# Row-tiled transposes of q and k, 64x128 tiles for the scores and the state's part, and a later place for u's transposes

## The chip, the cores and the metric

The kernel runs on one core of a Trainium2 chip. A core has five engines with instruction queues of their own: TensorE (PE, matrix products; the loading of its stationary operand is listed apart as PEld), VectorE (DVE), ScalarE (ACT), GpSimd (POOL) and SyncE (SP, which only issues transfers here). TensorE writes into PSUM, eight banks of 512 fp32 values for each of 128 partitions, and DVE and ACT read it from there. The metric is the device time of one execution in microseconds (us): 671.15 us as the median of 3 runs (670.82 to 672.76).

## The reference: what is computed

```python
# attention, B=4, H=8, S=768, D=64; a decay lam per head
for b in range(nb):                       # blocks of tokens
    intra = einsum('bhic,bhjc->bhij', qb, kb) * Dmask
    intra = einsum('bhij,bhjd->bhid', intra, vb)
    inter = einsum('bhid,bhde->bhie', qb * lam_pow, kv_state)
    out[:, :, sl] = intra + inter
    kv_state = lam_block * kv_state + einsum('bhsd,bhse->bhde', kb * rev_pow, vb)
# mixer, x = out as (4, 768, 512); rank 32, hidden 2048
h  = x.transpose(0, 2, 1) @ U @ V
u  = x + h.transpose(0, 2, 1)
return u + maximum(u @ w_ch1, 0) @ w_ch2
```

The first part is a causal linear attention with a state per head. The second adds a low-rank mix over the tokens and then a two-layer network over the 512 channels.

## The kernel before, in words

The kernel has three stages. The front stage (about the first 118 us) computes the attention and the low-rank mix, in 24 steps: step `s` is one tile of 128 tokens of one batch, six tiles to a batch (`NT = 6`, `c = s % NT`). The two later stages are the two large products with the weights (lines 733/743 and 866/868/870); they are not touched.

The order in the front stage is written out by hand: a list `pieces` (lines 562 to 584) names the pieces of each step, and every engine executes its own share strictly in that order. No planner moves anything. For step `s` TensorE gets, in this order:

- `prep(s+1)`, through `turn_half` (L355): the 8 heads of q and of k of the next tile, transposed two heads at a time on the full 128x128 array: four transposes into the PSUM bank `pq`, four into `pk`. ACT copies each bank to SBUF (`qt`, `kt`, L358).
- `mix(done)` with `done = s - 7` (L515): one 128x512 product into the bank `pu`; DVE adds it to the tile's attention result (L518). From then on the tile is u.
- At the first tile of a batch only (steps 6, 12, 18): `low(b-1)` (L470), the 24 products of the low-rank part, into `pp`. For batch 0 it lies in bank `pu`, later in bank `pq`. `low_rows` and two later pieces read it: DVE L490 and, behind the state's addition, DVE L496 (for batch 0 ACT copies it away first, L486).
- `intra(s)` (L453): masked scores times v into `px`, on 128x64 tiles; ACT copies it out (L459).
- `state(s)` (L418): decayed k times v into `pkv`, in bank `pk`; DVE adds it to the faded state (L426). Not in the last tile of a batch.
- `scores(s+1)` (L400): the scores of the next tile into the two banks `pss`. Up to step 6 on two 64x128 tiles of the array (rows x columns), after it on four 64x64 tiles.
- `inter(s+1)` (L441): the state's part of the next tile, q scaled (`qs`, by POOL, L383) times the state, into `px`, on four 64x64 tiles. Not in the first tile of a batch, which has no state.
- `turn(done)` (L532): four 128x128 transposes of u into the bank `pt`, and behind them SP's store of u to DRAM. DVE splits the result (L537, L548).

`masked(s+1)` (DVE, L409) multiplies the scores with the decay mask and frees `pss`. `aside` holds steps that prepare weights, mostly on DVE. A one-off beginning (`keep_busy`, `pl`) runs a few products on zeros and spreads `lam`.

fp32 products take two passes through the array, so the profile counts two records for each; transposes have one.

Of the kernel before, what the change touches and what calls it, by code (L numbers as in the profile page):

```python
# [8 lines left out]
FP32 = mybir.dt.float32  # L9
# [5 lines left out]
P = 128  # L15
# [3 lines left out]
def kernel(  # L19
# [28 lines left out]
    nc = tc.nc  # L48

    B, H, S, D = q.shape  # L50
    HP = H // 2
    NT = S // P
    C = H * D
# [9 lines left out]
    TG = N // P  # L63
# [5 lines left out]
    FG = (NS - NT - 1) // TG  # L69
# [24 lines left out]
    u_d = [dram.tile([P, C], FP32, name=f"u_d{s}") for s in range(NS)]  # L94
# [151 lines left out]
    att = att_ctx.enter_context(tc.tile_pool(name="att", bufs=1))  # L246
# [14 lines left out]
    def bank(shape, name, tag):  # L261
        return psa[0].tile(shape, FP32, tag=tag, bufs=2, name=name)
# [3 lines left out]
    raw = {}  # L266

    def parts(s):
        return 2 if s == 0 else 1
# [23 lines left out]
    ident = keep.tile([P, P], FP32, name="ident")  # L293
# [40 lines left out]
    xs = {}  # L334
    st = {}
    kv = {}
    half = [slice(0, D), slice(D, P)]

    def keep_busy(n):

        out = one_bank([P, C], "idle", "pq")
        for i in range(n):
            nc.tensor.matmul(out=out[:, 0:P], lhsT=blank, rhs=blank, start=True, stop=True)  # L343

    qts, kts = {}, {}

    def turn_half(s, a0, name):

        ts, tag = (qts, ("pq", "pt")) if name == "q" else (kts, ("pk", "pu"))
        if a0 == 0:  # L350
            ts[s] = att.tile([P, HP, P], FP32, tag=name + "t", bufs=2, name=name + "t")
        n = HP // parts(s)
        pt = one_bank([P, n, P], "p" + name, tag[a0 > 0])
        for a in range(a0, a0 + n):
            nc.tensor.transpose(  # L355
                out=pt[:, a - a0, :], in_=raw[s, name][:, 2 * a : 2 * a + 2, :], identity=ident
            )
        nc.scalar.copy(ts[s][:, a0 : a0 + n, :], pt)  # L358

    def prep(s):  # L360
        for a0 in range(0, HP, HP // parts(s)):
            for name in "qk":
                turn_half(s, a0, name)
        st[s].update(qt=qts.pop(s), kt=kts.pop(s))
        for name in "qk":
            load_next(name)
# [27 lines left out]
    def scores(s):  # L394
        qt, kt = st[s]["qt"], st[s]["kt"]
        st[s]["pss"] = pss = two_banks("pss", "pss").rearrange("p x (a i) -> p x a i", a=HP)
        for a in range(HP):
            for x in range(2):
                for rows in half if s > NT else [slice(0, P)]:
                    nc.tensor.matmul(  # L400
                        out=pss[rows, x, a, :], lhsT=kt[half[x], a, rows],
                        rhs=qt[half[x], a, :], start=True, stop=True,
                    )

    def masked(s):
        pss = st[s].pop("pss")
# [4 lines left out]
    def state(s):  # L411
        c = s % NT
        if c < NT - 1:
            ks, vr = st[s]["ks"], raw[s, "v"]
            pkv = one_bank([P, HP, D], "pkv", "pk")
            for a in range(HP):
                for x in range(2):
                    nc.tensor.matmul(  # L418
                        out=pkv[half[x], a, :], lhsT=ks[:, a, x, :], rhs=vr[:, 2 * a + x, :],
                        start=True, stop=True,  # L420
                    )
            kv[s + 1] = att.tile([P, HP, D], FP32, tag="kv", bufs=2, name="kv")
            if c == 0:
                nc.vector.tensor_copy(out=kv[s + 1], in_=pkv)
            else:
                nc.vector.tensor_tensor(out=kv[s + 1], in0=pkv, in1=st[s]["faded"], op=ALU.add)  # L426
        del st[s]
        del raw[s, "v"]
        load_next("v")

    def inter(s):

        st[s]["px"] = both = two_banks("px", "px")
        px = both[:, :, 0 : HP * D].rearrange("p x (a e) -> p x a e", a=HP)
        if s % NT == 0:
            return

        for a in range(HP):
            for x in range(2):
                for t in range(2):  # L440
                    nc.tensor.matmul(  # L441
                        out=px[half[t], x, a, :], lhsT=st[s]["qs"][half[x], a, half[t]],
                        rhs=kv[s][half[x], a, :], start=(a == 0), stop=False,
                    )

    def intra(s):
        first = s % NT == 0
# [15 lines left out]

    def low(b):

        tag = "pq" if b else "pu"
        pp = one_bank([P, P], "pp", tag) if b < B - 1 else bank([P, P], "pp", "b2")
        for c in range(NT):
            for g in range(G):
                nc.tensor.matmul(  # L470
                    out=pp[g * R : (g + 1) * R, :], lhsT=u_w[:, c, :],
                    rhs=xs[b * NT + c][:, g * P : (g + 1) * P],
                    start=(c == 0), stop=(c == NT - 1),
                )
        pps[b] = pp
# [44 lines left out]
    uhl, ud, turned = {}, {}, {}  # L520
    hl_at, d_at = [hl_pool], [d_pool]

    def turn(s):

        g, n = divmod(s, TG)
        if n == 0:
            uhl[g] = hl_at[g >= FG].tile([P, 2, CT, N], F32R, tag="hl", name="u_hl")
            ud[g] = d_at[g >= FG].tile([P, CT, N], F32R, tag="d", name="u_d")
        cols = slice(n * P, (n + 1) * P)
        pt = one_bank([P, CT, P], "put", "pt") if g < FG else bank([P, CT, P], "put", "b1")  # L530
        for ct in range(CT):
            nc.tensor.transpose(  # L532
                out=pt[:, ct, :], in_=xs[s][:, ct * P : (ct + 1) * P], identity=ident
            )
        nc.sync.dma_start(out=u_d[s], in_=xs.pop(s))
        t = tmp("ut").rearrange("p (c n) -> p c n", n=P)
        nc.vector.tensor_scalar(t.bitcast(U32), pt.bitcast(U32), HI, None, ALU.bitwise_and)  # L537
        hi, low, diff = uhl[g][:, 0, :, cols], uhl[g][:, 1, :, cols], ud[g][:, :, cols]
        if g >= FG:

            nc.vector.scalar_tensor_tensor(diff, t, 1.0 + E, pt, ALU.mult, ALU.subtract)
            uf = tmp("uf").rearrange("p (c n) -> p c n", n=P)
            nc.scalar.mul(hi, t, E)
            nc.scalar.copy(uf, pt)
            nc.gpsimd.tensor_tensor(out=low, in0=uf, in1=t, op=ALU.subtract)
            return
# [16 lines left out]
    for s in range(NS):  # L563
        b, c = divmod(s, NT)
        done = s - NT - 1
        more = s + 1 < NS
        step = [("prep", s + 1), ("scale", s + 1)] * more + [("fade", s)] * (c == 1)
        step += [("late", s - 1)] * (s in (NT, 3 * NT - 1))
        step += [("mix", done)] * (0 <= done < NS - NT - 1)
        step += [("low", b - 1)] * (c == 0 and b > 0)  # L570
        step += [("low_rows", b - 1)] * (c == 0 and b > 0)
        step += [("intra", s)]
        step += [("next_of_low", b - 1)] * (c == 0 and b > 0)
        step += [("late", s)] * (s < NT - 1 or s == NT) + [("state", s)]
        step += [("next_of_low", b - 1)] * (c == 0 and b > 0)
        step += [("turned", done - 1)] * (done > 0) + [("late", s)] * (done >= 0)
        step += [("next_of_low", b - 1)] * (c == 0 and b > 0)
        step += [("scores", s + 1)] * more
        step += [("aside", s)] * (s >= 2 * NT)
        step += [("inter", s + 1), ("masked", s + 1)] * more  # L580
        step += [("fade", s + 1)] * (more and c > 0)
        step += [("aside", s)] * (s < 2 * NT)
        step += [("turn", done)] * (done >= 0 and done // TG < FG)
        pieces += step
    waiting = {name: list(range(NS)) for name in "qkv"}

    def load_next(name, engine=nc.sync):
# [5 lines left out]
        "prep": prep, "fade": fade, "scores": scores, "masked": masked, "inter": inter,  # L593
        "intra": intra, "state": state,
        "low": low, "low_rows": low_rows, "next_of_low": next_of_low, "mix": mix, "turn": turn,
        "scale": scale, "turned": lambda s: turned.pop(s)(),
    }
    def v_steps():
# [371 lines left out]
```

## Time and profile before

| | |
|---|---|
| median of 3 runs | 671.15 us |
| profiled execution | 671.76 us, its span 669.9 us |
| PE, busy | 663.9 us (99%) |
| DVE, busy | 497.5 us (74%) |
| ACT, busy | 277.5 us (41%) |
| POOL, busy | 112.1 us (17%) |
| first matmul of the large products (L733) | at 118.99 us |
| DVE busy in 50 to 62, 62 to 74, 98 to 110 us | 10.81, 11.55, 11.87 of 12 us |
| transposes of q and k (L355), 192 records | 30.6 us of PE records |
| inter (L441), 640 records | 13.3 us of PE records |
| scores (L400), 656 records | 28.1 us of PE records |

Records of matmuls overlap, since several tiles of the array work at once, and their ends are modelled. What a group costs is therefore read from the start of one group to the start of the next, not from the sum of its records. The timeline gives those starts.

### The profile page before, as it was taken

The page shows a single profiled execution, that of the slowest core. Times are in us where ns is not written, and L with a number is a line of the kernel's source. Part 1 is how long each engine was busy: PE and PEld are TensorE (multiplying, and loading weights), DVE is VectorE, ACT ScalarE, POOL GpSimd, SP SyncE. Part 2 cuts the span into 40 slices and gives each one's busy share as a digit, 9 for nine tenths or more (in the row PEclk, how much of TensorE's full clock was granted, in tenths as well). Part 3 has the DMA queues.
Part 4 walks back from the last instruction along what each step waited for, and adds up shares of the span by engine and source line. Part 5 has one row for each costly group of instructions (what it writes and reads, how often), then busy time and mean ns, then how long its engine had stood idle before and what let it go on. Part 6 is the DMA issues. An engine that isn't in the chain of part 4 may idle for free.

```text
span 669.9 us, 13328 instructions
## 1 busy us (share of the span) xinstructions
PE 663.9 (99%) x5204; PEld 544.5 (81%) x5204; DVE 497.5 (74%) x873; ACT 277.5 (41%) x517; POOL 112.1 (17%) x92
## 2 busy tenths in 40 slices
PE   9999999999999999999999999999999999999997
PEld 8898989788888888888888888888888888888886
DVE  4689989877999777777797265787586775865864
ACT  4675866454655444444454122232322322322320
POOL 4455767240000000000000000030030300300300
PEclk9999999999999999999999999999999999999999
DMA  8999894354776655555577989854363353543421
GB/s 188 219 234 248 212 246 141 102 196 153 262 251 233 215 202 202 201 202 204 204 282 273 326 308 392 282 184 136 95 220 95 118 196 95 160 155 94 163 90 63
DMA packets 131776, 131.29 MB, mean 196 GB/s; under 512 B 81346, under 2 KB 89794, under 8 KB 131714
## 3 DMA queue, kind: packets, MB, share of 16 engines
q1 hardware_dynamic: 130512, 130.05, 61.1%
q8 instruction: 41, 0.67, 0.4%
q10 hardware_dynamic: 1202, 0.39, 0.2%
q14 instruction: 21, 0.17, 0.1%
HBM read 80.09 MB, written 50.33 MB: 195 GB/s over the span
## 4 chain that ended last, share of the span: by engine, by line
PE 97%; DVE 1%; DMA 1%; ACT 0%; issue 0%; DVEq 0%; ACTq 0%
PE pz L733 27%; PE pz L868 13%; PE pz L866 13%; PE pd L743 13%; PE pd L870 13%; PE px L453 4%; PE pss L400 3%; PE put L532 2%; PE pq L355 2%; PE pkv L418 1%; PE pk L355 1%; PE px L441 1%; DMA qraw<-in_q_dram 1%; PE pp L470 1%; PE pu L515 1%; PE idle L343 0%
## 5 line engine op out<-in xcount | busy, mean ns | idle before, releaser
L733 PE MATMUL pz<-u_hl,w 128*128 128x512 f32 x768 | 190.5, 397 | 0.0
L733 PEld LDWEIGHTS pz<-u_hl,w 128*128 128x128 f32 x768 | 144.0, 188 | 35.4 <-issue 0.4
L868 PE MATMUL pz<-w_hl,m 128*128 128x512 f32 x384 | 151.1, 396 | 0.0
L866 PE MATMUL pz<-w_hl,m 128*128 128x512 f32 x384 | 150.9, 396 | 0.0
L870 PE MATMUL pd<-w_d,m 128*128 128x512 f32 x384 | 149.5, 396 | 0.0
L849 ACT ACTIVATE m<-mt 128x512 fp32r<-128x512 f32 x96 | 60.5, 632 | 196.4 <-PE pd L870 140.9
L850 DVE SCALAR_TENSOR_TENSOR m<-rm,m 128x512 fp32r<-128x512 f32 x96 | 71.4, 746 | 53.8 <-ACT m L849 53.5
L895 POOL TENSOR_TENSOR o<-o,u 128x512 f32<-128x512 f32 x20 | 29.9, 1527 | 447.4 <-DVE o L891 447.4
L748 DVE SCALAR_TENSOR_TENSOR r<-pd,r 128x512 f32<-128x512 f32 x96 | 61.8, 686 | 53.6 <-ACT r L739 43.5
L743 PE MATMUL pd<-u_d,w 128*128 128x512 f32 x384 | 98.6, 397 | 0.0
L739 ACT ACTIVATE r<-pz 128x512 f32<-128x512 f32 x96 | 52.2, 596 | 93.2 <-PE pz L733 92.5
L868 PEld LDWEIGHTS pz<-w_hl,m 128*128 128x128 f32 x384 | 72.3, 188 | 17.7
L870 PEld LDWEIGHTS pd<-w_d,m 128*128 128x128 f32 x384 | 72.3, 188 | 17.6
L866 PEld LDWEIGHTS pz<-w_hl,m 128*128 128x128 f32 x384 | 72.3, 188 | 17.6
L743 PEld LDWEIGHTS pd<-u_d,w 128*128 128x128 f32 x384 | 72.1, 188 | 17.3
L851 DVE SCALAR_TENSOR_TENSOR m<-m 128x512 fp32r<-128x512 f32 x96 | 69.1, 721 | 0.9
L848 DVE TENSOR_SCALAR mt<-rm 128x512 uint32<-128x512 uint32 x96 | 46.1, 481 | 26.4 <-DMA rm<-r_d 26.1
L409 DVE TENSOR_TENSOR sm<-pss,mask 128x512 f32<-128x512 f32 x48 | 30.9, 685 | 7.3 <-PE pss L400 7.1
L212 ACT CAST w<-wt 128x512 fp32r<-128x512 f32 x32 | 19.9, 620 | 30.6 <-DVE wt L209 23.4
L383 POOL TENSOR_TENSOR qs<-qt,powq 128x512 f32<-128x512 f32 x20 | 25.9, 1297 | 20.3 <-ACT qt L358 19.8
L453 PEld LDWEIGHTS px<-vraw,sm 128*64 128x64 f32 x768 | 24.6, 137 | 5.5 <-issue 2.3
L453 PE MATMUL px<-vraw,sm 128*64 128x64 f32 x768 | 28.1, 225 | 0.1
(88 smaller groups left out, 682.1 us busy)
## 6 DMA issues: line engine op xcount, KB each, us to landing
r_d<-r SPq DMA_DIRECT2D x96, 256.0 KB, 2.4
rm<-r_d SPq DMA_DIRECT2D x96, 256.0 KB, 2.7
words<-in_moe_w_ch_dram SPq DMA_DIRECT2D x30, 512.0 KB, 4.5
w_d<-w SPq DMA_DIRECT2D x16, 768.0 KB, 3.3
w_hl<-w_d SPq DMA_DIRECT2D x16, 512.0 KB, 6.3
vraw<-in_v_dram SPq DMA_DIRECT2D x24, 256.0 KB, 5.0
u_d<-x_nat SPq DMA_DIRECT2D x24, 256.0 KB, 3.7
u<-u_d SPq DMA_DIRECT2D x24, 256.0 KB, 4.0
```

What stands on the lines that cost most here:

```text
L453: nc.tensor.matmul(out=px[half[t], x, a, :], lhsT=sm[:, x, a, half[t]], rhs=vr[:, 2 * a + x, :], start=(first and a == 0), stop=(a == HP - 1),
L733: nc.tensor.matmul(out=acc[g][0], lhsT=w[:, n, ct, :], rhs=uhl[g][:, n, ct, :], start=(ct == 0 and n == 0), stop=(ct == CT - 1 and n == 1),)
L739: nc.scalar.mul(rs[g], acc[g][0], 4096.0 + 1.0)
L743: nc.tensor.matmul(out=acc[g][1], lhsT=w[:, 2, ct, :], rhs=ud[g][:, ct, :], start=(ct == 0), stop=(ct == CT - 1),)
L748: nc.vector.scalar_tensor_tensor(rs[g], acc[g][1], 4096.0, rs[g], ALU.mult, ALU.add)
L848: nc.vector.tensor_scalar(t.bitcast(U32), r.bitcast(U32), HI, None, ALU.bitwise_and)
L849: nc.scalar.activation(out=m[:, 0], in_=t, func=AF.Relu)
L850: nc.vector.scalar_tensor_tensor(m[:, 1], r, 0.0, hi, ALU.max, ALU.subtract)
L851: nc.vector.scalar_tensor_tensor(m[:, 2], hi, E, low, ALU.mult, ALU.subtract)
L866: nc.tensor.matmul(out=pz, lhsT=m[:, 0, cols], rhs=hl[:, 0], start=first, stop=False)
L868: nc.tensor.matmul(out=pz, lhsT=m[:, 1, cols], rhs=hl[:, 1], start=False, stop=end)
L870: nc.tensor.matmul(out=pd, lhsT=m[:, 2, cols], rhs=dd, start=first, stop=end)
```

## The change

Four things are changed; all other code, the loads and the large products stay.

1. `turn_parts` takes the place of `turn_half`. Each transpose of 128 tokens becomes two of 64 tokens, on the two row tiles of the array (64 rows, 128 columns); their results go to two banks. q and k of a tile share one pair of banks, `pqk`. ACT still makes two copies of 128x512.
2. `scores` uses the 64x128 tiles in all steps, and `inter` has 8 products on 64x128 tiles in place of 16 on 64x64 tiles. The transposes that follow `inter` work on the same shape of tiles.
3. u's transposes (`turn`) move from the end of step `s` to the next step, behind `prep`. The store of u to DRAM keeps its place, as a piece `store` of its own.
4. Banks: `pkv` lies in `pqk` now, `pp` (batches 0 to 2) in `pss`, `idle` in `pt`, `pl` in `pqk`; the second half of the very first tile's transposes goes to `pss`.

```diff
-    def turn_half(s, a0, name):
-        ts, tag = (qts, ("pq", "pt")) if name == "q" else (kts, ("pk", "pu"))
+    def turn_parts(s, a0):
+        n = HP // parts(s)
         if a0 == 0:
-            ts[s] = att.tile([P, HP, P], FP32, tag=name + "t", bufs=2, name=name + "t")
-        n = HP // parts(s)
-        pt = one_bank([P, n, P], "p" + name, tag[a0 > 0])
-        for a in range(a0, a0 + n):
-            nc.tensor.transpose(
-                out=pt[:, a - a0, :], in_=raw[s, name][:, 2 * a : 2 * a + 2, :], identity=ident
-            )
-        nc.scalar.copy(ts[s][:, a0 : a0 + n, :], pt)
+            for ts, name in ((qts, "qt"), (kts, "kt")):
+                ts[s] = att.tile([P, HP, P], FP32, tag=name, bufs=2, name=name)
+        pt = two_banks("pqk", "pss" if a0 else "pqk")[:, :, 0 : 2 * n * D]
+        pt = pt.rearrange("p t (n a i) -> p t n a i", n=2, a=n)
+        for i, name in enumerate("qk"):
+            for a in range(n):
+                for t in range(2):
+                    nc.tensor.transpose(
+                        out=pt[:, t, i, a, :],
+                        in_=raw[s, name][half[t], 2 * (a0 + a) : 2 * (a0 + a) + 2, :],
+                        identity=ident[half[t], half[t]],
+                    )
+        for i, ts in enumerate((qts, kts)):
+            nc.scalar.copy(
+                ts[s][:, a0 : a0 + n, :].rearrange("p a (t i) -> p t a i", t=2), pt[:, :, i]
+            )
@@ scores
-                for rows in half if s > NT else [slice(0, P)]:
-                    nc.tensor.matmul(
-                        out=pss[rows, x, a, :], lhsT=kt[half[x], a, rows],
-                        rhs=qt[half[x], a, :], start=True, stop=True,
-                    )
+                nc.tensor.matmul(
+                    out=pss[:, x, a, :], lhsT=kt[half[x], a, :], rhs=qt[half[x], a, :],
+                    start=True, stop=True,
+                )
@@ state
-            pkv = one_bank([P, HP, D], "pkv", "pk")
+            pkv = two_banks("pkv", "pqk")[:, 0, 0 : HP * D].rearrange("p (a e) -> p a e", a=HP)
@@ inter
-                for t in range(2):
-                    nc.tensor.matmul(
-                        out=px[half[t], x, a, :], lhsT=st[s]["qs"][half[x], a, half[t]],
-                        rhs=kv[s][half[x], a, :], start=(a == 0), stop=False,
-                    )
+                nc.tensor.matmul(
+                    out=px[:, x, a, :], lhsT=st[s]["qs"][half[x], a, :],
+                    rhs=kv[s][half[x], a, :], start=(a == 0), stop=False,
+                )
@@ low
-        tag = "pq" if b else "pu"
-        pp = one_bank([P, P], "pp", tag) if b < B - 1 else bank([P, P], "pp", "b2")
+        pp = two_banks("pp", "pss")[:, 0, 0:P] if b < B - 1 else bank([P, P], "pp", "b2")
@@ turn, and the order of the pieces
+    def store(s):
+        nc.sync.dma_start(out=u_d[s], in_=xs[s])
-        nc.sync.dma_start(out=u_d[s], in_=xs.pop(s))
+        if g >= FG:
+            store(s)
+        del xs[s]
         step += [("late", s - 1)] * (s in (NT, 3 * NT - 1))
+        step += [("turn", done - 1)] * (done > 0 and (done - 1) // TG < FG)
         step += [("mix", done)] * (0 <= done < NS - NT - 1)
...
-        step += [("turn", done)] * (done >= 0 and done // TG < FG)
+        step += [("store", done)] * (done >= 0 and done // TG < FG)
@@ the beginning
-        out = one_bank([P, C], "idle", "pq")
+        out = one_bank([P, C], "idle", "pt")
-    pl = one_bank([P, H], "pl", "pt")
+    pl = two_banks("pl", "pqk")[:, 0, 0:H]
```

On DVE, ACT, POOL and SP the instructions keep their order, the two copies of a tile's transposes (now 128x2x4x64) included. On PE only the groups named above change shape or place.

More of the change, by code (lines that the diff above doesn't have):

```diff
@@ L345 @@
     qts, kts = {}, {}
-    def turn_half(s, a0, name):
-        ts, tag = (qts, ("pq", "pt")) if name == "q" else (kts, ("pk", "pu"))
+    def turn_parts(s, a0):
+        n = HP // parts(s)
         if a0 == 0:
-            ts[s] = att.tile([P, HP, P], FP32, tag=name + "t", bufs=2, name=name + "t")
-        n = HP // parts(s)
-        pt = one_bank([P, n, P], "p" + name, tag[a0 > 0])
-        for a in range(a0, a0 + n):
-            nc.tensor.transpose(
-                out=pt[:, a - a0, :], in_=raw[s, name][:, 2 * a : 2 * a + 2, :], identity=ident
+            for ts, name in ((qts, "qt"), (kts, "kt")):
[13 more added lines that the diff above has]
+                ts[s][:, a0 : a0 + n, :].rearrange("p a (t i) -> p t a i", t=2), pt[:, :, i]
             )
-        nc.scalar.copy(ts[s][:, a0 : a0 + n, :], pt)
     def prep(s):
         for a0 in range(0, HP, HP // parts(s)):
-            for name in "qk":
-                turn_half(s, a0, name)
+            turn_parts(s, a0)
         st[s].update(qt=qts.pop(s), kt=kts.pop(s))
@@ L595 @@
         "low": low, "low_rows": low_rows, "next_of_low": next_of_low, "mix": mix, "turn": turn,
+        "store": store,
         "scale": scale, "turned": lambda s: turned.pop(s)(),
```

## The prediction

> **What bounds the kernel now.** I read the page first, the busy times and the chain that ended last:
>
> ```profile
> PE 663.9 (99%) x5204; PEld 544.5 (81%) x5204; DVE 497.5 (74%) x873; ACT 277.5 (41%) x517; POOL 112.1 (17%) x92
> ...
> PE 97%; DVE 1%; DMA 1%; ACT 0%; issue 0%; DVEq 0%; ACTq 0%
> ```
>
> TensorE's queue sets the end, also in the front stage. Whatever lengthens or shortens the front on PE moves all that follows, so the sum is made of PE time up to the first product of L733 at 118.99 us. Next the PE timeline, here of one whole step (start, us of records, group):
>
> ```profile
> 42.12 1.10 PE L400 MATMUL pss<-qt,kt 64*64 64x128 f32 x32
> 43.04 0.64 PE L441 MATMUL px<-kv,qs 64*64 64x64 f32 x32
> 43.62 0.66 PE L532 MATMUL put<-ident,x_nat 128*128 128x128 f32 x4
> 44.11 0.60 PE L355 MATMUL pq<-ident,qraw 128*128 128x128 f32 x4
> 44.55 0.60 PE L355 MATMUL pk<-ident,kraw 128*128 128x128 f32 x4
> 44.90 0.47 PE L515 MATMUL pu<-vp 128*128 128x512 f32 x1
> 45.30 1.15 PE L453 MATMUL px<-vraw,sm 128*64 128x64 f32 x32
> 46.28 0.64 PE L418 MATMUL pkv<-vraw,ks 128*64 128x64 f32 x16
> 46.85 1.10 PE L400 MATMUL pss<-qt,kt 64*64 64x128 f32 x32
> ```
>
> A step takes 46.85 - 42.12 = 4.73 us with no gap. I count in rounds, one record on every tile of the array at once. L453: 16 rounds in 0.98 us, less 0.05 for its first load: 58 ns, at 64 moving columns. L355: 4 in 0.44: 109 ns at 128. L418: 8 rounds of 58 ns are 0.464 of its 0.57, so a change of tile shape costs 0.106. Third, the weight loads by form (12 to 58 us; busy, mean ns):
>
> ```profile
> L441 PEld LDWEIGHTS px<-kv,qs 64*64 64x64 f32 x320 | 5.8, 134 | 0.6
> L400 PEld LDWEIGHTS pss<-qt,kt 64*128 64x128 f32 x83 | 5.2, 187 | 0.3
> ...
> L355 PEld LDWEIGHTS pk<-ident,kraw 128*128 128x128 f32 x40 | 4.7, 142 | 0.0
> ```
>
> Beside 110 ns for 32 columns (L470, same view), a load grows by 0.8 ns a column: about 53 ns of loading for 64, 107 for 128. A transpose's load of 128 columns takes 142, like one of 64. The load of the next round runs under the present one, so a round lasts as long as the longer of load and stream. The early steps show the one form in which 128 columns are loaded on row tiles:
>
> ```profile
> 28.61 1.16 PE L400 MATMUL pss<-qt,kt 64*128 64x128 f32 x16
> 29.70 0.69 PE L441 MATMUL px<-kv,qs 64*64 64x64 f32 x32
> ```
>
> 1.09 us less 0.107 (first load) and 0.106 (change of shape) is 8 rounds of 110 ns; I use 111.
>
> Last, what reads `pp`, in DVE's and PE's timelines at steps 12 and 18 (two answers):
>
> ```profile
> 67.11 1.10 PE L400 MATMUL pss<-qt,kt 64*64 64x128 f32 x32
> 67.23 0.42 DVE L424 COPY kv<-pkv 128x256 f32<-128x256 f32 x1
> ...
> 67.69 1.25 DVE L496 TENSOR_TENSOR vp<-pp,p_h 32x128 fp32r<-32x128 f32 x4
> ```
>
> ```profile
> 96.39 1.10 PE L400 MATMUL pss<-qt,kt 64*64 64x128 f32 x32
> ...
> 96.97 1.25 DVE L496 TENSOR_TENSOR vp<-pp,p_h 32x128 fp32r<-32x128 f32 x4
> ```
>
> DVE finishes with `pp` at 68.94 and 98.22, 1.83 us after the next scores began. Today nobody minds.
>
> **What the skill says.** The Trainium skill's "TensorE: Matmul & The Clock Gate", section "LDWEIGHTS (loading the stationary operand)", prices a load at its columns / 1.2 ns whatever its rows: 53 and 107 ns, as the trace has it. The same page's "Terms" calls the transposes' load four times faster for fp32; the trace shows twice (142 against 187, of which some 84 is not loading). "TensorEngine Tiling (Array Packing)", "Restrictions", says column tiling takes this mode away; the new transposes use all 128 columns, and no run here shows it on row tiles. Its "Key Properties" has a change of mode drain the array: the 0.106 above.
>
> **The change part by part.**
>
> *Transposes.* Before, 8 rounds of 109 = 0.872 us a tile. After, 16 transposes, two at once, are 8 rounds with 64 moving columns and a fast load of about 57: 8 x 58 = 0.464. Gain 0.408. Bounds: 58, and 111 if on row tiles the load runs as the scores' does (loss 0.016). I take 58, since the load's rate shows no dependence on rows (64*64 and 128*64 both 134 to 138).
>
> *inter.* Before, 8 rounds of 58 = 0.464. After, 8 products of two passes on two tiles are again 8 rounds, now with 128 columns to load for 64 to stream: bound by loads, 8 x 111 = 0.888. Loss 0.424. Bounds 58 and 111; I take 111, which the early scores pay for the same load.
>
> *Scores* after step 6: 8 x 111 + 0.107 for 8 x 109 + 0.053: loss 0.070.
>
> *Changes of shape.* In a full step three before (to 128x64, to 64x64, to 128x128) and three after (128x64, 64x128, 128x128 for u): no gain. In steps 1 to 5, without u, four become two: gain 0.21.
>
> A full step thus loses 0.424 + 0.070 - 0.408 = 0.086 us. A step 1 to 5 goes from 2.74 (28.61 to 31.35) to 0.107 + 0.888 + 0.888 + 0.464 + 0.106 = 2.45: gain 0.29, at most 0.2 after the wait for the mask (1.2 to 2.5 us behind the scores' start, against intra at 2.45).
>
> *Edits at nothing.* ACT's copies stay 0.58 each and may start after q's part; ACT has them done some 3.5 us after the scores' start, `pkv` in `pqk` needs them at 3.4 (early steps; up to 0.1 uncovered) or 4.2. u's later place delays DVE's L537 to L518 by some 0.9 us, into idle time before them; PE reads their result a step later. The store keeps its place in SP's queue, loads theirs. `idle`, `pl`, and the first tile's second half in `pss` (scores there need all four ACT copies) precede the wait for qraw at 17.46, which takes early gains anyway.
>
> *pp in pss, step 6.* `low` must now wait for `masked(6)`, which runs on DVE behind 2.9 us of weight work from 34.03 to 35.32. The early gain reaches DVE as about 0.8 (0.39 from the transposes after qraw's arrival, 0.2 for each of two steps), so `pp` can start at 35.37 - 0.8 = 34.57, against 34.55 before. All early gains end in this wait: net 0, bounds -0.3 and +0.4.
>
> *Steps 7 to 11.* In step 7 `pu` waits for ACT (L505) and hides the loss; then four steps x 0.086 = +0.34.
>
> *Step 12.* Scores(13) must wait until L496 has read `pp`, and behind it on PE stand inter, the next transposes, everything. DVE works without a gap from the mask to L496, so it is late by what PE is: end at 68.94 + 0.34, plus 0.07 to hand over: 69.35 for 67.11. Now +2.24 (PE would be ready at 66.9: `pp` from the mask's end at 63.85, then 1.45 + 0.98 + 0.57). The gain of 0.41 on the transposes in this step vanishes in the wait.
>
> *Steps 13 to 17.* 5 x 0.086: +2.67. *Step 18.* Likewise: 98.22 + 2.67, less 0.35 that DVE waits today for `pp` and `pkv` (0.13 and 0.22), plus 0.07: 100.61 for 96.39: +4.22. *Steps 19 to 22.* +0.34. *Step 23* has inter but no transposes after it: +0.49. **Sum +5.1 us**: the profiled execution goes from 671.76 to 676.9 (span 675.0), and as that execution lies 0.6 over the median of the runs, the median from 671.15 to 676.2.
>
> **The rivals.**
>
> *A, inter's loads don't bind* (not slower). If two row tiles load 128 columns under 64 streamed ones at 58 ns, 14 steps after 7 save 0.424 each: 5.1 - 5.9 = -0.8, 670.4. The scale is linear: no loss below 65 ns a round, within 0.3% (about 2 us, what a measurement of this kernel can tell) below 83. Against it: the 110 ns of the early scores are a little above the 109 of a pure stream, as a load-bound round would be, but there both are long, so the trace doesn't separate them.
>
> *B, the transposes' fast load is lost on row tiles.* 111 ns a round: +0.424 in some 14 steps that PE bounds (8 to 11, 13 to 18, 19 to 22): +5.9, so 682.1. For it: no row-tiled transpose in the trace. Against: loads at equal columns cost the same at 64 and 128 rows.
>
> *C, the wait for pp is short.* If DVE reached L496 right behind PE's state, the two waits (1.9 and 1.55) vanish and the two steps keep their 0.34 from the transposes: 5.1 - 1.9 - 1.55 - 0.68 = +1.0, 672.1. Against: DVE's 11.55 of 12 us there, and seven groups from the mask (L409) to L424 ahead of L496 in its order.
>
> *D, further cost*: PE idle for over 2 us twice may lower its clock, which the skill's clock page (Part 1) puts at half after some 3.4 us of idleness; the trace shows no such gap. Or DVE's lateness reaches intra through the mask, with one buffer. 1 to 4 us more: 678 to 681.
>
> **How the numbers follow.** My case 0.58, B 0.14, D 0.10, C 0.08, A 0.10. The predicted time is that of my case, 676.2, whose own range is 674.3 to 678 (0.4 at step 6, 0.5 in each wait, 15 ns on inter's rounds). The range leaves out A and a part of C and of B's upper side: 672.0 to 682.6. Faster by over 0.3% needs A and a small wait: 0.03. Within 0.3%: most of A and of C: 0.14. Slower: 0.83.
>
> **What would show it.** Right: the 8 transposes of q (L358 then) start 0.23 before those of k; L446 takes 0.89 from its start to the next group's; loads of `px<-kv,qs` near 187 ns, of the transposes near 142; PE waits on DVE L500 (L496 before) of about 2.4 and 1.6 us at the scores of tiles 13 and 19, nowhere else over 0.5 but before `pp`; first L744 product at 124. Wrong: inter's group at 0.5 to 0.6 (A), transposes at 0.9 a tile (B), no wait at the two scores (C), a stage clock below full (D).

## The result, and the profile after

The changed kernel takes 681.8 us (median of 4 runs, 680.85 to 682.37) where the kernel before takes 671.68 (670.82 to 672.76): a ratio of 1.0148, 95% interval 1.0128 to 1.0169. It is slower by 10.1 us; 5.1 were forecast. The time lies in the range that was given, but above 678, where the likeliest case's own range ended. The profiled execution went from 671.76 to 681.63 us, its span from 669.9 to 679.8. From the page, busy times and the chain that ended last:

```profile
PE 666.0 (98%) x4804; PEld 547.6 (81%) x4804; DVE 497.8 (73%) x873; ACT 277.8 (41%) x517; POOL 111.9 (16%) x92
...
PE 95%; DVE 3%; ACT 1%; DMA 1%; issue 0%; ACTq 0%; DVEq 0%
```

DVE's share of the chain rose from 1 to 3%: PE now waits for it. The first product of the large weights (L744, L733 before) starts at 128.83 us for 118.99. These 9.84 us are the whole loss, since from there to the end of the span the kernels take 550.9 and 551.0. The table has it by stretches between the starts of the scores (PE timeline; a stretch "step s" runs from scores(s) to scores(s+1)):

| stretch | before, us | after, us | more | forecast |
|---|---|---|---|---|
| start to scores(6) | 32.44 | 32.81 | +0.37 | -0.8 |
| steps 6 and 7 | 9.68 | 10.86 | +1.18 | +0.8 |
| steps 8 to 11 | 18.47 | 18.81 | +0.34 | +0.34 |
| step 12 | 6.52 | 9.22 | +2.70 | +1.90 |
| step 13 | 4.75 | 6.41 | +1.66 | +0.09 |
| steps 14 to 17 | 18.68 | 18.70 | +0.02 | +0.34 |
| step 18 | 5.85 | 7.51 | +1.66 | +1.55 |
| step 19 | 4.74 | 6.27 | +1.53 | +0.09 |
| steps 20 to 22 | 14.38 | 14.41 | +0.03 | +0.26 |
| step 23 to L744 | 3.48 | 3.83 | +0.35 | +0.49 |

A whole step, in the PE timeline after the change (start, us of records, group):

```profile
48.55 1.16 PE L406 MATMUL pss<-qt,kt 64*128 64x128 f32 x16
49.54 1.01 PE L446 MATMUL px<-kv,qs 64*128 64x64 f32 x16
50.38 0.42 PE L358 MATMUL pqk<-ident,qraw 64*128 64x64 f32 x8
50.63 0.42 PE L358 MATMUL pqk<-ident,kraw 64*128 64x64 f32 x8
50.98 0.66 PE L539 MATMUL put<-ident,x_nat 128*128 128x128 f32 x4
51.39 0.47 PE L519 MATMUL pu<-vp 128*128 128x512 f32 x1
51.79 1.15 PE L458 MATMUL px<-vraw,sm 128*64 128x64 f32 x32
52.77 0.64 PE L424 MATMUL pkv<-vraw,ks 128*64 128x64 f32 x16
53.34 1.16 PE L406 MATMUL pss<-qt,kt 64*128 64x128 f32 x16
```

The step takes 4.79 us, against 4.73. `inter` needs 0.84 from its start to the next group's; the transposes 0.25 for q and 0.35 for k, the change of shape in it. The loads on 12 to 58 us, by form (busy, mean ns):

```profile
L446 PEld LDWEIGHTS px<-kv,qs 64*128 64x128 f32 x144 | 9.0, 188 | 0.2 <-issue 0.2
...
L358 PEld LDWEIGHTS pqk<-ident,kraw 64*128 64x128 f32 x80 | 3.5, 139 | 0.0
```

`inter`'s loads of 128 columns take 188 ns, and the row-tiled transposes keep their fast load, at 139. So the tile shapes cost what was forecast, and the steps between the waits are not where the loss is. It is around tiles 13 and 19 (timeline of PE, two stretches; in brackets the idle time before the group and what ended it):

```profile
65.34 1.52 PE L474 MATMUL pp<-x_nat,u_w 128*32 128x128 f32 x48 [0.39 <-DVE sm L415]
66.79 1.15 PE L458 MATMUL px<-vraw,sm 128*64 128x64 f32 x32
67.77 0.64 PE L424 MATMUL pkv<-vraw,ks 128*64 128x64 f32 x16
71.70 1.90 PE L406 MATMUL pss<-qt,kt 64*128 64x128 f32 x16 [3.29 <-DVE vp L500]
73.38 1.82 PE L446 MATMUL px<-kv,qs 64*128 64x64 f32 x16
74.98 0.57 PE L358 MATMUL pqk<-ident,qraw 64*128 64x64 f32 x8
...
78.11 1.16 PE L406 MATMUL pss<-qt,kt 64*128 64x128 f32 x16
```

```profile
104.32 1.16 PE L406 MATMUL pss<-qt,kt 64*128 64x128 f32 x16 [1.80 <-DVE vp L500]
105.31 1.13 PE L446 MATMUL px<-kv,qs 64*128 64x64 f32 x16
106.23 0.65 PE L358 MATMUL pqk<-ident,qraw 64*128 64x64 f32 x8
106.66 0.64 PE L358 MATMUL pqk<-ident,kraw 64*128 64x64 f32 x8
107.23 1.11 PE L539 MATMUL put<-ident,x_nat 128*128 128x128 f32 x4
```

Two things are to be seen. Before each of these scores PE stands idle, for 3.29 and 1.80 us, until DVE's L500 has read `pp` out of `pss`. And behind the wait the same groups take longer: scores 1.68 from start to start for 1.00, `inter` 1.60 for 0.84, u's transposes 0.77 for 0.41. The same time cut into stretches of one microsecond, around both places (behind the length come the busy us of PE, PEld, DVE, ACT and POOL with their counts of instructions, then PE's granted clock, the DMA share and GB/s):

```profile
71.00:72.00 1.00, 0.30 (x4) 0.30 (x6) 0.58 (x2) 0.96 (x3) 0.09 (x1) 0.97 0.62 226
72.00:73.00 1.00, 1.00 (x14) 1.00 (x14) 0.00 (x0) 0.47 (x1) 1.00 (x1) 0.50 0.06 18
...
74.00:75.00 1.00, 1.00 (x14) 1.00 (x14) 0.92 (x2) 0.00 (x0) 0.00 (x0) 0.50 0.00 0
75.00:76.00 1.00, 1.00 (x20) 0.93 (x20) 0.00 (x0) 0.10 (x1) 0.00 (x0) 0.83 0.00 0
```

```profile
106.00:107.00 1.00, 1.00 (x22) 1.00 (x20) 0.82 (x2) 0.00 (x0) 0.00 (x0) 0.53 0.07 16
107.00:108.00 1.00, 1.00 (x11) 0.88 (x8) 0.00 (x0) 0.66 (x2) 0.00 (x0) 0.50 0.02 5
...
109.00:110.00 1.00, 1.00 (x32) 1.00 (x30) 0.97 (x3) 0.50 (x3) 0.28 (x1) 0.76 0.17 36
```

The clock is halved for about 3.4 us each time: a value of 0.97 means that 0.06 of that microsecond ran at half, so, worked out from the slices, the half clock lasts from 71.94 to 75.34, and from 106.06 to 109.48. All four runs have a mean clock of 0.995 or 0.996, so this is not one unlucky execution. Steps 13 and 19 lose 1.6 and 1.5 us by it.

The other new place is step 6 (PE timeline):

```profile
33.81 0.41 PE L358 MATMUL pqk<-ident,qraw 64*128 64x64 f32 x8
34.05 0.41 PE L358 MATMUL pqk<-ident,kraw 64*128 64x64 f32 x8
35.92 1.52 PE L474 MATMUL pp<-x_nat,u_w 128*32 128x128 f32 x48 [1.46 <-DVE sm L415]
```

### The profile page after: what moved, and what is told of

The parts are those of the page before. It is cut to its first block, busy times and chain, and to the rows that moved or that the text cites. A ratio compares the mean times of both kernels' runs of the same rounds, so it can differ in the third digit from the quotient of the medians.

```text
span 679.8 us, 12534 instructions
## 1 busy us (share of the span) xinstructions
PE 666.0 (98%) x4804; PEld 547.6 (81%) x4804; DVE 497.8 (73%) x873; ACT 277.8 (41%) x517; POOL 111.9 (16%) x92
## 4 chain that ended last, share of the span: by engine, by line
PE 95%; DVE 3%; ACT 1%; DMA 1%; issue 0%; ACTq 0%; DVEq 0%
PE pz L744 27%; PE pz L879 13%; PE pz L877 13%; PE pd L754 13%; PE pd L881 13%; PE pss L406 4%; PE px L458 3%; PE px L446 3%; PE put L539 2%; PE pqk L358 2%; PE pkv L424 1%; DVE sm L415 1%; PE pu L519 1%; PE pp L474 1%; DMA kraw<-in_k_dram 1%; ACT qt L364 0%
## 5 line engine op out<-in xcount | busy, mean ns | idle before, releaser
L744 PE MATMUL pz<-u_hl,w 128*128 128x512 f32 x768 | 190.3, 397 | 0.0
L744 PEld LDWEIGHTS pz<-u_hl,w 128*128 128x128 f32 x768 | 144.0, 188 | 35.3 <-ACT r L750 0.3
L406 PE MATMUL pss<-qt,kt 64*128 64x128 f32 x384 | 29.5, 296 | 6.0 <-DVE vp L500 5.1
L406 PEld LDWEIGHTS pss<-qt,kt 64*128 64x128 f32 x384 | 24.7, 197 | 7.9 <-DVE vp L500 5.4
```

The source lines that it names most:

```text
L406: nc.tensor.matmul(out=pss[:, x, a, :], lhsT=kt[half[x], a, :], rhs=qt[half[x], a, :], start=True, stop=True,)
L744: nc.tensor.matmul(out=acc[g][0], lhsT=w[:, n, ct, :], rhs=uhl[g][:, n, ct, :], start=(ct == 0 and n == 0), stop=(ct == CT - 1 and n == 1),)
```

## The experiments

Times are medians; each kernel is compared with the kernel before on the same chip (671.7 to 672.9 us there).

**Is it the hold of `pp` in `pss`?** The first experiment changes the condition in `low_rows`, so that ACT copies `pp` away for batches 1 and 2 too, as it does for batch 0, and L500 reads the copy:

```diff
-        if b == 0:
+        if b < B - 1:
```

> The changed kernel, but the low-rank result of batches 1 and 2 is first copied out of pss by ScalarE (four copies of 32x128, 0.26 us each), as batch 0 has it; DVE then reads the copy. Theory (two holds of pss, and the clock halved for 3.4 us after each): the scores of tiles 13 and 19 start right behind the state's part, no clock below full between 70 and 112 us, and the 2.7 + 1.6 + 1.7 + 1.5 us that steps 12 and 18 lost are gone: about 674.5. Rival (DVE is the bound of these steps, the hold only shows it): DVE is as late as before, the wait moves to the mask or to pp, and at most 2 to 3 us come back: 679.

Measured: 675.79 us, ratio 1.0075 (1.0054 to 1.0096); from scores(6) to the first large product 89.70 us for 96.02. All waits of PE between 30 and 122 us (in all, times, longest):

```profile
PE pp L474 <- DVE sm L415: 2.0, 3, 1.5
PE px L446 <- DVE kv L430: 0.9, 1, 0.9
```

The waits at the scores are gone, and the clock is 1.0 throughout. A part of them comes back one group later, where `inter` of tile 13 waits 0.87 for the state that DVE is late with; step 13 takes 6.16 us for the 4.80 of the whole steps behind it. So the hold, with what follows from it, is worth some 6 of the 10 us.

The second does the same to the kernel before: only `pp` of batches 0 to 2 is put into `pss`, everything else stays.

```diff
-        tag = "pq" if b else "pu"
-        pp = one_bank([P, P], "pp", tag) if b < B - 1 else bank([P, P], "pp", "b2")
+        pp = two_banks("pp", "pss")[:, 0, 0:P] if b < B - 1 else bank([P, P], "pp", "b2")
```

> The kernel before, with pp (batches 0 to 2) in pss and nothing else changed. Theory: the scores of tiles 13 and 19 wait 1.9 us each for DVE, pp of tile 6 waits 0.8 us for the mask: +4.4, and the clock may halve after each stretch of 1.9 us without products, 1.5 us more each: between 676 and 679. Rival (the hold costs only in combination with the new shapes): +1, 672.7.

Measured: 676.35 us, 1.0061 (1.004 to 1.0082), first large product at 123.01 for 118.99 us. PE waits 0.8 before `pp` of step 6, then 2.2 and 1.8 at the scores of tiles 13 and 19; steps 6, 12 and 18 take 0.90, 1.47 and 1.74 longer than before, 4.1 in sum. The clock stays full: the hold alone costs 4 us.

**Is it the clock?** The third keeps the waits of the changed kernel and fills them: 13 and 7 products of the identity with itself into the free bank `pt`, ahead of the scores of tiles 13 and 19. Their results are used by nobody.

```diff
+    def fill(s):
+        out = one_bank([P, C], "idle", "pt")
+        for i in range(13 if s == 2 * NT else 7):
+            nc.tensor.matmul(out=out[:, 0:P], lhsT=ident, rhs=ident, start=True, stop=True)
...
+        step += [("fill", s)] * (s in (2 * NT, 3 * NT))
         step += [("scores", s + 1)] * more
...
```

> The changed kernel, with 13 and 7 products of the identity with itself (about 2.9 and 1.5 us) put into TensorE's two waits ahead of the scores of tiles 13 and 19. They add no result. Theory (the idle stretch halves the clock afterwards, and the half clock costs 1.6 and 1.5 us): both waits keep their ends (scores at 71.7 and 104.3 or a little earlier), the clock stays at 1.0 throughout, and 3 us come back: 678.8. Rival (the slow stretches have another cause, such as the matmuls' operands or transfers): no change or up to 1 us more: 682 to 683.

Measured: 679.06 us, 1.0116 (1.01 to 1.0131). PE timeline of step 12 to 13:

```profile
69.22 3.17 PE L348 MATMUL idle<-ident 128*128 128x128 f32 x26
72.59 1.16 PE L411 MATMUL pss<-qt,kt 64*128 64x128 f32 x16 [0.21 <-DVE vp L505]
73.59 1.01 PE L451 MATMUL px<-kv,qs 64*128 64x64 f32 x16
```

The scores still start 9.23 us behind those of tile 12 (9.22 in the changed kernel), so the wait is as long as it was; but scores and `inter` have their usual lengths again, and the first large product comes 3.09 us sooner behind scores(6). Useless work makes the kernel faster, by 3.1 us in the trace and 2.7 in the medians: so much of the loss is the clock.

**Why is DVE late in step 12?** The forecast wait was 2.4, the measured one 3.29. One row of DVE's timeline differs (the changed kernel; 0.68 us in the kernel before), and POOL's timeline shows what runs beside it:

```profile
65.11 1.74 DVE L191 SCALAR_TENSOR_TENSOR wf<-m,sc 128x512 f32<-128x512 f32 x1
```

```profile
65.03 1.27 POOL L390 TENSOR_TENSOR qs<-qt,powq 128x512 f32<-128x512 f32 x1
```

L191 and POOL's scaling of q both read two operands in SBUF. POOL starts 0.08 us sooner and ends at 66.30; L191 ends 0.55 after that, as if it had begun its 0.68 about there. In the seven other kernels below and above in which `qs` starts ahead of L191, by 0.07 to 0.23 us, it is the same: L191 ends 0.54 to 0.56 us behind `qs`. The Trainium skill's "SBUF — State Buffer", section "SBUF: two separate sides", says that a DVE operation with two SBUF inputs and a POOL operation that reads SBUF share a port pair as an exclusive lock: who starts first has it to the end, and the other waits in full. Before, `qs` started 3.55 us behind scores(12), after L191 was done; now that q's transposes stand ahead of u's, it starts 2.55 behind, just where L191 (2.6 to 2.8 behind) begins. The test swaps POOL's two instructions of that step, so that `qs` comes behind the waiting `ks`:

```diff
     def scale(s):
+        if s == 2 * NT + 1:
+            scale_k(s + 1)
         if s % NT > 0:
...
-        if s + 1 < NS:
+        if s + 1 < NS and s != 2 * NT + 1:
             scale_k(s + 1)
```

> The changed kernel with POOL's two instructions of tile 13's preparation in the other order: first ks of tile 14, which waits until about 68.5 us, then qs of tile 13, so that qs no longer starts just ahead of DVE's L191 in step 12. Nothing else is changed; inter of tile 13 still finds its qs in time if that is done by about 71. Theory that L191 is held up by qs: L191 takes 0.68 to 0.76 us instead of 1.74, DVE is through with pp about 1.0 earlier (70.6), the wait at the scores of tile 13 falls from 3.29 to about 2.3, and those scores start at about 70.7 instead of 71.7. Time: 680.8 if TensorE's clock is halved after that wait as before, 679.2 if a wait of 2.3 there no longer brings the half clock. Rival, that L191 is slow because of what else moves at that time (transfers, its own operands): it stays at 1.7, the wait at 3.3, time 681.8.

Measured: 678.7 us (678.29 to 679.89), 1.009 (1.0068 to 1.0112). DVE's timeline, and PE's:

```profile
66.12 0.68 DVE L191 SCALAR_TENSOR_TENSOR wf<-m,sc 128x512 f32<-128x512 f32 x1
```

```profile
71.66 1.16 PE L407 MATMUL pss<-qt,kt 64*128 64x128 f32 x16 [2.24 <-DVE vp L501]
72.65 1.01 PE L447 MATMUL px<-kv,qs 64*128 64x64 f32 x16
```

L191 is back at 0.68 and the wait is shorter by 1.05, step 12 now 8.17 us long. That `qs` holds up L191 is shown, and with it the size of the wait. (In this execution all lies some 1.3 us later from the second tile on.) In the profiled execution the clock stayed full after both waits, the unchanged one of 1.80 us too, which no theory had expected; that gave another 3.1 us in steps 13 and 19. It is not sure to do so: two of the four runs have a mean clock of 0.997, which fits one half clock of 3.4 us.

**Is moving u's transposes free?** Only the move and the piece `store`, applied to the kernel before:

```diff
...
+        step += [("turn", done - 1)] * (done > 0 and (done - 1) // TG < FG)
         step += [("mix", done)] * (0 <= done < NS - NT - 1)
...
-        step += [("turn", done)] * (done >= 0 and done // TG < FG)
+        step += [("store", done)] * (done >= 0 and done // TG < FG)
```

> The kernel before, with u's transposes behind those of q and k of the next step, and the store as a piece of its own; nothing else. Theory (the move costs nothing, DVE has the idle time): the full steps stay at 4.73 us and the time within 0.3% of the kernel before. Rival (DVE gets u later and passes it on to the mask or to pp): PE waits of 0.3 us and more a step, +4.

Measured: 674.48 us, 1.0034 (1.002 to 1.0049); the profiled execution had 672.76, its first large product at 120.05, 1.06 later than before. So the move is not free. The six runs go from 672.51 to 674.88, and two of them have a mean clock of 0.996; the trace shows one of the fastest, and explains only a part of the 2.8 us of the medians. Whole steps stay at 4.74. DVE's timeline and PE's, step 12 to 13:

```profile
63.00 1.64 DVE L191 SCALAR_TENSOR_TENSOR wf<-m,sc 128x512 f32<-128x512 f32 x1
```

```profile
68.30 0.69 PE L441 MATMUL px<-kv,qs 64*64 64x64 f32 x32 [1.22 <-DVE kv L424]
69.49 0.66 PE L355 MATMUL pq<-ident,qraw 128*128 128x128 f32 x4 [0.49 <-DVE vp L496]
```

The same collision, without any new tile shape: `qs` starts at 62.80, L191 takes 1.64, and what DVE is late with now holds up `inter`. In all kernels of this study it goes the same way: L191 took 1.59 to 1.75 wherever `qs` had started first, 0.68 to 0.76 wherever it had not; and where L191 came first by 0.17 us, in the two kernels with 64x64 scores below, it was `qs` that took 1.73 and 1.74 for 1.28.

**Do `inter`'s loads bind?** The kernel before with `inter` alone on 64x128 tiles:

```diff
-                for t in range(2):
-                    nc.tensor.matmul(
-                        out=px[half[t], x, a, :], lhsT=st[s]["qs"][half[x], a, half[t]],
-                        rhs=kv[s][half[x], a, :], start=(a == 0), stop=False,
-                    )
+                nc.tensor.matmul(
+                    out=px[:, x, a, :], lhsT=st[s]["qs"][half[x], a, :],
+                    rhs=kv[s][half[x], a, :], start=(a == 0), stop=False,
+                )
```

> The kernel before, with inter alone on 64x128 tiles (8 products in place of 16). Theory (128 columns of weights to load bound a round of 64 streamed ones at 111 ns): inter's group takes 0.89 us in place of 0.46, and behind scores on 64x64 tiles one more change of shape and a longer first load come to it, 0.2 us: 0.6 us in each of 15 steps, about +9: 680.5. Rival A (a load hides under the streams of the other row tile, 58 ns a round): only the change of shape, +1.5 to +3: 673.5.

Measured: 680.99 us, 1.0141 (1.0123 to 1.0159). PE timeline:

```profile
49.52 1.11 PE L440 MATMUL px<-kv,qs 64*128 64x64 f32 x16
50.56 0.66 PE L531 MATMUL put<-ident,x_nat 128*128 128x128 f32 x4
```

`inter` takes 1.04 us for 0.58, and a whole step 5.31 for 4.73. The 0.58 are 8 rounds of 111 for 58 ns (0.424), one more change of shape and a longer first load. Rival A falls.

**Can step 6 be mended?** `pp` of batch 0 back in the bank `pu`, in the changed kernel:

```diff
-        pp = two_banks("pp", "pss")[:, 0, 0:P] if b < B - 1 else bank([P, P], "pp", "b2")
+        if b == 0:
+            pp = one_bank([P, P], "pp", "pu")
+        else:
+            pp = two_banks("pp", "pss")[:, 0, 0:P] if b < B - 1 else bank([P, P], "pp", "b2")
```

> The changed kernel, but the low-rank result of batch 0 lies in the bank pu, as before the change. Theory: the wait of 1.46 us at step 6 is pp's wait for the mask's reading of pss; without it pp runs inside that time and intra of step 6 starts at about 36.0, not 37.37; the rest follows 1.4 us earlier: 680.4. Rival (the mask itself is late, and intra needs it as well): intra waits for the mask instead, less than 0.4 us comes back: 681.5.

Measured: 680.25 us, 1.0133 (1.0115 to 1.0151). Step 6 takes 4.59 us for 6.11, but step 7 5.48 for 4.75, because `inter` of tile 7 now waits 0.81 for the state from DVE. Only 0.8 is left of 1.5; DVE, which prepares weights just there, is what binds. The time fell by more than that: the wait of 3.29 at tile 13 was not followed by a half clock in this execution (step 13 4.81), that of 1.80 at tile 19 was (6.27).

Both repairs together, the one of the first experiment and this one:

> The changed kernel with both repairs: ScalarE copies pp out for batches 1 and 2, and pp of batch 0 lies in pu. Theory: what is left against the kernel before is 0.09 for each full step (about 1.3), 0.35 at step 23, 0.05 in each early step and the waits of 0.4, 0.2 and 0.9 for mask and state: about +3, 675. Rival (the repairs cost what they gain, since DVE is late): as with the copy alone, 676.

Measured: 674.81 us (12 runs), 1.0036 (1.0022 to 1.005). What is left are two waits of `inter` for DVE (0.81 and 0.87), 0.6 before `pp`, and a step 22 of 5.34 us for 4.80.

**Can the shapes be had without `inter`'s loss?** `scores` and `inter` on 64x64 tiles as before, in the changed kernel:

```diff
-                nc.tensor.matmul(
-                    out=pss[:, x, a, :], lhsT=kt[half[x], a, :], rhs=qt[half[x], a, :],
...
+                for rows in half:
+                    nc.tensor.matmul(
+                        out=pss[rows, x, a, :], lhsT=kt[half[x], a, rows],
...
-                nc.tensor.matmul(
-                    out=px[:, x, a, :], lhsT=st[s]["qs"][half[x], a, :],
...
+                for t in range(2):
+                    nc.tensor.matmul(
+                        out=px[half[t], x, a, :], lhsT=st[s]["qs"][half[x], a, half[t]],
...
```

> The changed kernel with scores and inter on four 64x64 tiles in all steps; the transposes on row tiles, u's place and the banks stay. Theory (the transposes gain 0.41 a step, inter and scores lose 0.42 and 0.07, a change of shape between inter and the transposes costs 0.11): a full step falls from 4.80 to about 4.42, and about 5 us come back, the holds of pss and the half clocks staying: 677. Rival (DVE, busy for 93% of these steps, is the next bound): PE waits at the mask or at pp instead, less than 2.5 us comes back: 679.5.

Measured: 678.85 us (675.17 to 680.71, 10 runs), 1.0091 (1.007 to 1.0113). In the profiled execution whole steps take 4.5 to 5.0 us, one 6.5, because PE stands idle where nothing is late ("issue"), once for 1.6 us; seven of the ten runs have a mean clock of 0.997. The same shapes with both repairs and with `pkv` of the first five tiles in `pu`:

```diff
+            if s < NT - 1:
+                pkv = one_bank([P, HP, D], "pkv", "pu")
+            else:
+                pkv = two_banks("pkv", "pqk")[:, 0, 0 : HP * D]
```

> Both repairs, pkv of tiles 0 to 4 in the free bank pu, and scores and inter on 64x64 tiles: what is kept of the change is the transposes on row tiles and u's later place. Theory: 0.30 a step under the kernel before (0.41 of the transposes less one change of shape), 16 to 20 steps, less the waits for the mask at pp: -3 to -5, 668. Rival (DVE becomes the bound): the step stays near 4.7 and the time within 1 us of 671.7.

Measured: 675.31 us (12 runs), 1.0046 (1.003 to 1.0062), 7 us above what the theory had said, with such gaps in the middle of a group:

```profile
75.18 0.57 PE L452 MATMUL px<-kv,qs 64*64 64x64 f32 x21 [1.01 <-issue]
```

By the counts in the timeline these kernels have 133 records of matmuls in a whole step, the kernel before 125, the changed one 101. The next has 117: both repairs, `pkv` likewise, `scores` on 64x128 and only `inter` on 64x64:

> Both repairs, pkv of tiles 0 to 4 in pu, the transposes on row tiles, scores on 64x128 tiles, inter on 64x64 tiles: 32 fewer records of matmuls and loads a step than with the scores on 64x64 tiles. Theory (the gaps put down to issue there came from the number of TensorE's instructions in a stretch with busy DMA engines): no gap put down to issue over 0.3 us on PE, a full step of 4.60 to 4.68 and 671 to 673. Rival (they come from the changes of tile shape, of which this has as many): gaps as before, 674 to 676.

Measured: 672.96 us (20 runs), 1.0021 (1.0013 to 1.0028). No gap of this kind between 30 and 122 us, whole steps of 4.72. So the gaps don't come from changing the tile shape within a step, which this kernel does more often; they appear with the larger number of instructions. What holds PE there isn't shown. This is the best version found, and it is no faster than the kernel before. The L191 collision (1.59) is still in it, and `inter` waits 0.9 for DVE; it was not run with the swap on POOL.

With `inter` on 64x128 in it too, that is the changed kernel with both repairs and `pkv` of five tiles in `pu`:

> Both repairs, and pkv of tiles 0 to 4 in the free bank pu; the shapes are those of the changed kernel. Theory (pkv's four waits of 0.3 us for ScalarE's copy of kt come from its place in pqk): steps 1 to 4 last 4.05 us in place of 4.34, and up to 1.2 us come back, as far as the mask of step 6 passes them on: 673.8. Rival (the mask or the loads of k bound these steps): nothing, 674.8.

Measured: 674.71 us, 1.0043 (1.0028 to 1.0058), no better than without the `pkv` edit (674.81). The edit shows what the early steps are worth: they fall from 4.34 to 3.98 us as long as the loads keep up, and then

```profile
32.49 1.15 PE L462 MATMUL px<-vraw,sm 128*64 128x64 f32 x32 [1.31 <-DMA vraw<-in_v_dram]
```

## Why the prediction was right and wrong

In short, the two mechanisms of the sum came as told: `inter`'s loads bind, and PE waits twice for `pp`. Three of its terms failed. The clock behind the waits stood at nothing and cost 3.0 us. Moving u's transposes stood at nothing and cost 0.8 in step 12. And the early steps, which were to gain 0.8 and so to pay for `pp`'s wait in step 6, lost 0.4. That the time still lies in the range is luck: its upper end had been set for rival B, which did not come.

*The tile shapes: right.* `inter` loses what its loads cost (0.84 measured for 0.89), the transposes' fast load holds on row tiles, and a whole step is longer by 0.065 (4.795 for 4.73) where 0.086 was forecast. Rivals A and B fall, A by an experiment of its own, B by the 139 ns. (The prediction's "twice" compares single loads. A product in fp32 has two of them in these views and a transpose one, so by the prediction's own figures it is 2 x 103 against 58 ns, some 3.5 times, close to the four named there.) Steps 8 to 11 cost the forecast 0.34. Steps 14 to 17 and 20 to 22 cost almost nothing, since steps 16 and 21 take 4.94 and 4.91 us in the kernel before, some 0.2 over their neighbours, and 4.79 to 4.81 in the changed one: a cover that the sum had not looked for.

*The hold of `pp` in `pss`: the mechanism right, steps 12 and 18 too.* PE waits there for DVE's L500 and nowhere else in steps 8 to 22 for more than 0.5. Step 18 was forecast at +1.55 and is +1.66. Rival C, a short wait, falls with the 3.29 and 1.80.

*The clock: the term that failed most.* The sum held a nought for what an idle stretch does to the work after it; rival D had it at 0.10. Step 13 was taken as +0.086 and is +1.66, step 19 likewise and is +1.53: 3.0 of the 4.8 us by which the sum fell short of the trace. The filling experiment gives 3.1 for it. With 2.4 and 1.6 us of idleness in the forecast, the term deserved more than that 0.10, but not certainty: waits of 2.2 and 1.8 us passed without it in other executions (last section). So a part of the 3.0 us hangs on where the waits happened to fall. (D's 678 to 681 counts from the 676.9 of the profiled execution; from the median's 676.2 its 1 to 4 us give 677 to 680.)

*Step 12: mis-sized, by the edit "at nothing".* It was +1.90 and is +2.70. The prediction moved u's transposes at no cost because DVE had idle time before the instructions that would come later; it followed DVE and SP, but not POOL. By the move q's transposes come first, `qs` starts 1.0 sooner behind the scores, and locks out L191 for 1.05 us. The swap on POOL takes this back: step 12 is 1.05 us shorter with it.

*Steps 1 to 6: the gain that was to pay for the wait did not come.* Steps 1 to 5 were to gain 0.2 each, and step 6 was to come out at nought. Steps 1 to 4 take 4.33 to 4.34 us, where three of them took 4.29 before and one 4.59, because `pkv` in `pqk` waits for ACT's copy of `kt`; "up to 0.1 uncovered" is 0.3 a step (the view of waits, 0 to 135 us; in all, times, longest):

```profile
PEld pkv L424 <- ACT kt L364: 1.1, 4, 0.3
```

And the first scores wait 0.74 for the same copy, which stood at nothing too. So DVE reaches the mask of tile 6 at 34.49 us, 0.46 later than before, where 0.8 sooner was reckoned with, and `pp` behind it starts at 35.92 for a forecast of 34.57. This is +1.35. Step 7, where `pu`'s wait was to hide the loss, adds 0.2: at scores(8) +1.55 for 0.

A part of this is again the clock, at the start of the execution. The first scores take 1.91 us from start to start before and 1.86 after, where later ones of this shape take 1.09 and 1.00: they run at half clock. The trace's clock record begins, with the full clock, at 8.08 us before and only at 10.49 after. The transposes behind these scores show it (PE timeline after the change; 0.43 us from start to start for the 0.25 of a whole step, while before they have their usual 0.49):

```profile
8.58 0.64 PE L358 MATMUL pqk<-ident,qraw 64*128 64x64 f32 x8
9.01 0.64 PE L358 MATMUL pqk<-ident,kraw 64*128 64x64 f32 x8
```

The transposes of q that before waited for their load until 17.46 start at 17.92, so 0.46 of the 1.35 was lost ahead of them, to the first waits and to this clock, which the runs don't separate. From there to the transposes of tile 7, at 33.81 (33.53 before), the kernel gains 0.18 where the sum had 0.8; that is mostly `pkv`. The late clock comes with the change: the ten profiled executions with row-tiled transposes have their full clock from 9.99 to 12.97 us on, the four others from 7.34 to 8.08. The waits of 0.29 and 0.74 in front of the first scores may be the reason; that was not tested. The 1.3 us by which the execution with the swap on POOL lies later fit it: its full clock begins at 12.88.

Together: +1.55 in the early steps, +3.0 by the clock behind the waits, +0.8 in step 12, +0.1 in step 18, less 0.7 in the later whole steps and the end, are the 4.8 us between 5.05 and 9.84.

*What stays open:* how much work in a window keeps the clock full, why the full clock begins later with the new transposes, and what holds up PE in the kernels with 133 records of matmuls a step.

## What to carry to other kernels

Price an idle stretch of TensorE of 1.8 us and more with the half clock that may follow it (1.5 to 1.7 us each here), not only with its own length. When a move lets an engine start something sooner, look at what every other engine runs at that moment: here a DVE operation with two operands in SBUF and one of POOL shut each other out, and the loser was on the critical path. And an early gain pays for a later wait only if it reaches the engine that ends the wait; here ACT's copies, DVE's weight work and the loads each took it on the way.

## What the hardware showed that was not expected

Both stretches of half clock last one and the same time, 3.40 and 3.42 us by the slices above, and they begin 34.12 us apart, at 71.94 and 106.06: ten times 3.41. The full clock's beginning at 10.49 lies 18 times 3.41 ahead of the first. The two also begin 0.24 us after PE's return in one case and 1.74 in the other. This agrees with the Trainium skill's "TensorE: Matmul & The Clock Gate", Part 1, which has a window of 3413 ns that runs freely. But its table asks for a whole idle window, and here 1.80 us of idleness was enough.

The other traces can be cut into the same windows, counted from their own changes of clock. Here are those with the waits at tiles 13 and 19, first in the changed kernel, then in the one with `pp` of batch 0 in `pu`, whose waits are as long (the second number behind the window is PE's busy time, the count of its records behind that):

```profile
68.52:71.93 3.41, 0.23 (x4) 0.23 (x6) 2.88 (x10) 1.99 (x5) 1.08 (x2) 1.00 0.93 243
102.65:106.06 3.41, 1.74 (x32) 1.74 (x34) 2.02 (x6) 2.40 (x5) 2.33 (x2) 1.00 0.59 163
```

```profile
67.03:70.44 3.41, 1.58 (x51) 1.44 (x48) 3.25 (x9) 0.89 (x2) 1.06 (x1) 1.00 0.97 250
70.44:73.85 3.41, 1.96 (x36) 1.96 (x38) 2.02 (x7) 2.18 (x4) 1.27 (x1) 1.00 1.11 266
101.16:104.57 3.41, 1.63 (x30) 1.63 (x30) 2.00 (x6) 2.51 (x5) 2.33 (x2) 1.00 0.58 161
```

Half clock follows both windows of the first kernel and the last of the second. The wait of 3.29 us lies in one window in the first kernel; in the second a border at 70.44 cuts it in two, and the clock stays full. With `pp` in `pss` alone, and with the swap on POOL, the waits are cut so that PE is busy for at least 1.9 us of every window, and no half clock follows. So where a wait lies in the windows matters as much as its length. The busy time alone doesn't draw the line: 1.74 us with 32 records and 1.63 with 30 were followed by half clock, 1.58 with 51 was not. What is counted stays open: this is read from the traces afterwards, and no run was made to test it.
